# A new instruction order, the last g split in place, and late output copies and transfers shared out, in an attention and two-MLP kernel

## The chip, the core and the metric

One core of a Trainium2 chip runs the whole program. The metric is the device time of one execution in microseconds; several runs give a median. TensorE is called PE, VectorE DVE, ScalarE ACT, GpSimd POOL and SyncE SP.

## What is computed

Three stages follow each other, all in float32. Attention of 4 batches, 8 heads, 576 positions and 64 columns is the sum of a coarse part (means of 4 positions, softmax over 144 of them, each result repeated 4 times) and a local part (softmax over the 7 positions within 3 of the query). Its output, 2304 rows of 512, goes through

```python
def _moe_ref(x, w1, w2, w3, w_out):
    a = x @ w1
    b = x @ w2
    h = a * b @ w3
    return (h @ w_out)

def _moe2_ref(x, w1, w2, w3, w_out):
    h = np.maximum(np.maximum(x @ w1, x @ w2), x @ w3)
    return (h @ w_out)
```

with inner widths 1024 and 768. The weights arrive as float64 words and are converted on the chip.

## The kernel before, in words

**Tiling.** The 2304 rows are five chunks of N = 504 (the last has 288). Products split each operand into a rounded high part and a rest (split, lines 447 to 453: ACT makes the high part, DVE the rest) and are three matmuls (mm3, lines 455 to 458). The first stage loads and converts w_out and w3 and multiplies them (weights_product; float32 at lines 476 to 482 is one ACT and four DVE operations; the product is line 750), while down (lines 505 to 600) makes the coarse attention of one pair of heads and slab the local one. Then front and back do the first MLP chunk by chunk, halves_front and rest_front the second MLP's three products with a running maximum, and final_rest and final its last product. halves_front works on two chunks at a time, rest_front on the chunk of 288; both store their maximum g to memory (g_dram), from where final and final_rest load it. z of rest_front is zs[2], in a buffer of its own that nothing uses again.

**The end.** final(ch) takes a chunk of 504 in two halves of columns, with seven products in place of eight and sums of them on DVE (t1, u2, t5, u3). put copies a result into output tiles whose columns are interleaved: one copy for each run of positions, each output tile T = 384 columns for one row group j, one half of the batches rd and one l of four. l = 0, 1 are the low tiles, 2, 3 the high ones. When the last copy into a tile is added, put adds its transfer (line 1002), 192 KB each, on SP's queue. In final the copies run on ACT. The last chunk's last product is cut into u = 0 and 1, both into one PSUM bank b1 (252 columns each); put for each has six copies of 12, 12, 96, 96, 24 and 12 columns, alternately on ACT and DVE (line 1107):

```python
for u in low:
    product(0, 2, x21, b1, False, (u,))
    put(b1, t0, n, [u], 0, u * n, ("ACT", "DVE"))
```

**The order.** Nothing is emitted where the code computes it. prog.add collects tasks (engine, cost, tiles read and written) and numbers them from 0; a tile may be given with a part, and then only accesses to the same part or to the whole tile depend on each other. ORDER, a table at the top, holds for each engine the task numbers in the order in which its queue runs them. Program.order simulates this with rough costs (AFTER: time from an engine's end to those who wait; RATE: bytes per us of the transfers; HAND, COME: PE's instructions at hand and their supply; PAUSE, HEAT: PE's clock), to choose among free buffers, and so decides which task is emitted next: the one that can start first. Each engine runs its queue in order; semaphores between the queues are set by the framework from the tiles that the emitted instructions touch, in the order of emission.

**Names used below.** Tasks 0 to 7 are warm-up matmuls (line 500). 20 is the first pair's scores (line 540); 221 and 222 load the two halves of the first part of w_out, 228 the first half of w3; 224 to 227, 231 to 234 and 236 to 239 are their DVE conversions; 315 is the first product of weights (line 750). For the second batch, 455 and 482 normalise the exponentials of head pairs 0 and 1 (line 570, ACT), 459/457 and 485/483 are pp and dp work (transposes on PE, line 579, copies on ACT, line 582; 457, 459 the copies of pair 0, 483, 485 the transposes of pair 1), 460 is the values product of pair 0 (line 589); 480 and 481 are DVE's sums and reciprocals of pair 1; 489 loads q and k of pair 2, and 497, 498 copy them (line 523, ACT). 609, 611, 615, 617 are the first four front products, 621 to 624 the first back products. At the end, before the change, 2557 and 2567 are the last product's u = 0 and 1, 2568 to 2576 the copies and transfers of u = 1 (2573 is the 24 columns on ACT, 2575 the last 12 on DVE); after it, they are 2547 and 2557, with 2558 to 2566, and 2542, 2544 and 2546 are the transfers of the high tiles.

## Time and profile before

| | us |
|---|---|
| three runs, lowest / median / highest | 746.69 / 749.17 / 751.23 |
| the profiled execution, its own time | 745.55 |
| its span, first to last instruction | 743.8 |
| PE busy in the span | 724.7 |
| DVE busy | 506.4 |
| ACT busy | 339.4 |

The span is 1.75 us shorter than the execution's own time. "Idle" and "waits" say how long an engine stood before an instruction and what ended that; busy times of PE are modelled from the records.

### The profile page before, as it was taken

The numbers are of one execution on the slowest core, as the hardware profiler recorded it, in microseconds if no ns is written. First come the engines' busy times: TensorE is split into PE (matmuls) and PEld (weight loads), VectorE is DVE, ScalarE is ACT, GpSimd is POOL, SyncE is SP. The second block draws the span as 40 slices with busy tenths as digits, with TensorE's granted clock in tenths as the row PEclk, the third lists the DMA queues.
The fourth block names the chain that finished last, engine by engine and source line by source line (L and its number), as shares of the span: only waits on it lengthen the run. The fifth ranks groups of instructions, "written<-read, shape, count | busy, mean of one in ns | idle before, by whom it ended". The sixth has DMA issues, their size and how long they took to land.

```text
span 743.8 us, 16204 instructions
## 1 busy us (share of the span) xinstructions
PE 724.7 (97%) x6636; PEld 578.0 (78%) x6636; DVE 506.4 (68%) x859; ACT 339.4 (46%) x744; POOL 48.6 (7%) x114
## 2 busy tenths in 40 slices
PE   6999999999999999999999999999999999999995
PEld 2445567777877777777888899888888888879995
DVE  6999988866253544354577699979846765468983
ACT  4865586555644573322443466432212311114775
POOL 2410104010310300000000000000000000000000
PEclk9999999999999999999999999999999999999998
DMA  9887854222432322012566496778593588586416
GB/s 333 277 248 228 262 175 109 84 50 68 104 82 68 64 75 60 21 34 53 186 238 253 173 309 226 271 265 273 221 363 111 196 286 269 200 295 225 143 46 223
DMA packets 64489, 133.31 MB, mean 179 GB/s; under 512 B 23520, under 2 KB 44000, under 8 KB 61344
## 3 DMA queue, kind: packets, MB, share of 16 engines
q1 hardware_dynamic: 59808, 128.74, 51.3%
q0 software_dynamic: 4608, 3.55, 3.4%
q8 instruction: 52, 0.85, 0.5%
q14 instruction: 21, 0.17, 0.1%
HBM read 90.57 MB, written 41.68 MB: 178 GB/s over the span
## 4 chain that ended last, share of the span: by engine, by line
PE 86%; DVE 8%; DMA 2%; ACT 1%; issue 1%; SPq 0%; DVEq 0%; ACTq 0%
PE pb L456 12%; PE pb L457 11%; PE pb L458 11%; PE pf L456 9%; PE pf L458 9%; PE pf L457 9%; PE py L456 5%; PE py L457 5%; PE py L458 5%; PE pw L750 3%; PE poq L688 2%; PE sq L643 2%; DVE wf L480 2%; DVE wf L482 1%; PE po L589 1%
## 5 line engine op out<-in xcount | busy, mean ns | idle before, releaser
L456 PE MATMUL pf<-xt,w 128*128 128x504 f32 (+1 forms) x320 | 121.0, 378 | 0.8 <-ACT dp L582 0.8
L456 PE MATMUL pb<-xc,wu 128*128 128x504 f32 (+1 forms) x324 | 120.7, 373 | 0.5
L457 PE MATMUL pb<-xc,wu 128*128 128x504 f32 (+1 forms) x324 | 119.8, 370 | 0.0
L458 PE MATMUL pb<-xc,wu 128*128 128x504 f32 (+1 forms) x324 | 119.5, 369 | 0.0
L458 PE MATMUL pf<-xt,w 128*128 128x504 f32 (+1 forms) x320 | 118.8, 371 | 0.0
L457 PE MATMUL pf<-xt,w 128*128 128x504 f32 (+1 forms) x320 | 118.8, 371 | 0.0
L456 PEld LDWEIGHTS pb<-xc,wu 128*128 128x128 f32 x324 | 60.8, 188 | 14.6 <-DVE t L912 4.7
L456 PEld LDWEIGHTS pf<-xt,w 128*128 128x128 f32 x320 | 60.1, 188 | 12.0 <-ACT dp L582 1.5
L458 PEld LDWEIGHTS pb<-xc,wu 128*128 128x128 f32 x324 | 60.9, 188 | 10.2
L457 PEld LDWEIGHTS pb<-xc,wu 128*128 128x128 f32 x324 | 60.9, 188 | 9.7
L458 PEld LDWEIGHTS pf<-xt,w 128*128 128x128 f32 x320 | 60.1, 188 | 10.4
L457 PEld LDWEIGHTS pf<-xt,w 128*128 128x128 f32 x320 | 60.2, 188 | 9.6
L782 DVE TENSOR_TENSOR z<-pf,z 128x504 f32<-128x504 f32 (+1 forms) x40 | 25.4, 635 | 60.0 <-PE pf L458 48.1
L912 DVE TENSOR_TENSOR t<-t,pb 128x504 f32<-128x504 f32 x60 | 40.4, 677 | 38.0 <-PE pb L458 19.9
L914 ACT COPY t<-pb 128x504 f32<-128x504 f32 x36 | 20.9, 581 | 97.8 <-PE pb L458 93.7
L456 PE MATMUL py<-g,wp 128*128 128x504 f32 (+1 forms) x160 | 63.6, 397 | 0.0
L750 PE MATMUL pw<-wf 128*128 128x512 f32 x128 | 58.8, 604 | 4.0 <-DVE wf L482 4.0
L457 PE MATMUL py<-g,wp 128*128 128x504 f32 (+1 forms) x160 | 59.5, 372 | 0.0
L458 PE MATMUL py<-g,wp 128*128 128x504 f32 (+1 forms) x160 | 59.4, 371 | 0.0
L456 PE MATMUL pb<-go,wm 128*128 128x252 f32 x168 | 46.9, 279 | 1.3 <-ACT area L996 1.3
L458 PE MATMUL pb<-go,wm 128*128 128x252 f32 x168 | 46.9, 279 | 0.0
L457 PE MATMUL pb<-go,wm 128*128 128x252 f32 x168 | 46.8, 278 | 0.0
(136 smaller groups left out, 1306.2 us busy)
## 6 DMA issues: line engine op xcount, KB each, us to landing
wu<-w_dram SPq DMA_DIRECT2D x18, 1024.0 KB, 7.6
w_dram<-hl SPq DMA_DIRECT2D x20, 512.0 KB, 3.0
qk<-qkp SPq DMA_DIRECT2D x16, 576.0 KB, 3.8
raw<-m SPq DMA_DIRECT2D x18, 512.0 KB, 3.7
raw<-w3t SPq DMA_DIRECT2D x16, 512.0 KB, 11.5
raw<-w SPq DMA_DIRECT2D x16, 512.0 KB, 4.5
w_dram<-hls SPq DMA_DIRECT2D x16, 512.0 KB, 3.6
m_dram<-hls SPq DMA_DIRECT2D x12, 512.0 KB, 5.4
```

What stands on the lines that cost most here:

```text
L456: nc.tensor.matmul(o, wlo, xhi, start=first, stop=False, skip_group_check=again)
L457: nc.tensor.matmul(o, whi, xlo, start=False, stop=False, skip_group_check=again)
L458: nc.tensor.matmul(o, whi, xhi, start=False, stop=last, skip_group_check=again)
L480: prog.add(dve(n), lambda e: e.scalar_tensor_tensor(u(), high(), 0xC0000000, u(), op0=ALU.bitwise_and, op1=ALU.bitwise_or), [words], cv)
L482: prog.add(dve(n), lambda e: e.scalar_tensor_tensor(u(), low(), 29, u(), op0=ALU.logical_shift_right, op1=ALU.bitwise_or), [words], cv)
L589: e.matmul(po()[a * D:(a + 1) * D, :GD], vd()[:, k, a * D:(a + 1) * D], pt()[:, k, a], start=(k == 0), stop=(k == 1),)
L643: e.matmul(sps[a]()[j * 32:(j + 1) * 32, (half * HP + hp) * BK:(half * HP + hp + 1) * BK], q[h, t:t + 32], k[h, t:t + BK], start=True, sto ...
L688: e.matmul(pos[hp]()[a * D:(a + 1) * D, i * BQ:(i + 1) * BQ], vw()[h, a, i], pt().rearrange("p a n -> p (a n)")[h, c:c + BQ], start=True, ...
L750: e.matmul(os[i](), w()[:, i * P:(i + 1) * P], o(), start=n == 0, stop=n == NF - 1)
L782: prog.add(psum(n), lambda e, pp=pp: e.tensor_tensor(z()[:, :n], pp()[:, :n], z()[:, :n], op=ALU.mult), [pp], [z])
L912: prog.add(dve(N), lambda e: e.tensor_tensor(ap(o), ap(x), ap(y), op=op), [x, y], [o])
L914: copy = lambda o, x: prog.add(act(N), lambda e: e.copy(ap(o), ap(x)), [x], [o])
```

## The change

It replaces ORDER on all engines (the task numbers from 2268 on shift, since ten transfers go), changes five constants of the planner, no longer stores and reloads g of f = 2 and 5 for the chunk of 288 but splits it from zs[2], shares put's copies of the last chunk between ACT and DVE, makes copies of b1 depend on half of it (part = u, also for the product that writes it), and stores the two high tiles of a row group with one transfer of 384 KB, from POOL's queue in the second half of the batches and from SP's in the first.

```diff
@@ ORDER["PE"] @@
-    "0 20 1 2 3 4 315 5 6 31 7 29 47 316 124 317 33 318 125 56 58 74 319 320 60 83 85 101 321 87 135 322 159 110 "
...
-    "615 617 621 622 460 623 624 625 627 485 631 632 633 483 634 501 635 637 641 551 642 643 644 552 645 487 510 "
...
-    "2408 2415 2423 2431 2462 2464 2466 2468 2474 2481 2491 2524 2526 2528 2530 2536 2543 2557 2567",
+    "0 1 20 2 3 4 5 315 6 29 7 31 47 316 124 317 33 318 125 58 56 74 319 320 60 83 85 101 321 135 87 322 159 112 "
...
+    "110 160 114 331 137 332 138 170 194 333 195 334 172 335 173 336 447 205 337 207 338 208 458 456 474 609 611 "
+    "615 617 460 483 485 621 622 623 624 625 627 631 501 632 633 634 635 551 637 641 552 642 643 644 487 512 645 "
...
+    "2404 2411 2419 2426 2457 2459 2461 2463 2469 2476 2484 2517 2519 2521 2523 2529 2536 2547 2557",
@@ ORDER["DVE"], its first and last lines @@
-    "18 19 236 237 22 21 238 239 224 225 231 226 227 232 233 234 248 249 250 251 26 27 45 241 46 242 243 244 269 "
...
-    "2507 2511 2475 2469 2476 2482 2513 2514 2516 2520 2518 2521 2529 2531 2523 2537 2538 2544 2565 2559 2561 "
-    "2569 2575 2571",
+    "18 19 236 22 237 238 21 231 232 239 233 234 224 225 226 227 248 45 249 26 27 250 46 251 241 242 243 244 49 "
...
+    "2503 2500 2504 2470 2471 2477 2506 2507 2511 2509 2513 2514 2522 2516 2524 2528 2530 2531 2535 2526 2533 "
+    "2537 2545 2539 2549 2555 2565 2541 2559 2551 2561",
@@ ORDER["ACT"], around tasks 455 and 482, and its last lines @@
...
-    "443 444 200 360 356 354 471 371 470 176 206 180 450 451 452 367 365 498 455 211 217 213 382 459 457 497 341 "
-    "219 343 339 477 478 376 479 610 524 345 613 616 525 387 378 389 619 393 482 400 461 626 486 398 629 484 404 "
-    "504 505 506 415 411 636 409 426 509 557 639 646 488 513 511 531 532 533 536 656 563 515 431 538 649 540 592 "
...
-    "2542 2551 2546 2547 2558 2535 2560 2563 2554 2548 2539 2545 2541 2573 2568 2570",
...
+    "282 130 82 61 86 303 104 105 84 106 289 136 88 109 325 323 329 113 111 327 115 296 310 165 349 141 444 145 "
+    "171 470 200 443 360 471 354 176 356 180 206 450 451 452 367 365 371 455 382 217 211 459 341 457 610 339 477 "
+    "478 479 345 343 482 378 616 389 376 613 387 619 497 393 498 461 404 486 626 524 484 504 505 525 506 398 409 "
+    "629 509 219 636 411 213 400 415 639 513 488 557 646 426 649 511 563 531 532 422 533 536 656 538 592 515 540 "
...
+    "2360 2518 2472 2295 2485 2515 2407 2492 2421 2410 2473 2312 2302 2525 2305 2474 2534 2527 2475 2491 2543 "
+    "2550 2532 2548 2553 2560 2558 2540 2563 2538",
@@ ORDER["POOL"], ORDER["SP"] @@
...
+    "1046 1048 1071 1124 1098 1125 1102 1100 1101 1099 1126 1072 2544 2546 2542",
-    "8 222 9 221 228 245 246 229 35 266 267 252 253 36 259 260 63 62 89 273 90 274 280 301 281 302 288 287 436 "
...
-    "2485 2484 2493 2552 2553 2562 2566 2564 2556 2550 2576 2574 2549 2555 2572",
+    "8 222 9 228 246 221 245 35 266 229 267 253 252 36 259 63 260 62 89 273 90 274 117 280 118 123 281 287 302 "
...
+    "2433 2269 2496 2495 2498 2494 2493 2497 2431 2430 2481 2487 2424 2479 2486 2490 2489 2556 2554 2566 2562 "
+    "2552 2564",
@@ -248,12 +248,12 @@
-    AFTER = {"PE": 0.16, "DVE": 0.12, "ACT": 0.15, "POOL": 0.15, "SP": 1.9}
-    RATE = 0.36e6
+    AFTER = {"PE": 0.16, "DVE": 0.12, "ACT": 0.15, "POOL": 0.15, "SP": 2.3}
+    RATE = 0.33e6
     ADDS, MORE = 2.2, 4.5
 
-    HAND, COME = 165, 70
-    BEGIN, PAUSE, HEAT = 0.8, 4.2, 4.5
+    HAND, COME = 165, 45
+    BEGIN, PAUSE, HEAT = 0.8, 3.8, 4.5
 
     def __init__(self):
         self.tasks, self.chains, self.group = [], {}, 0
@@ -967,14 +967,14 @@
                 prog.add(act(n), lambda e, i=i, pp=pp: e.copy(z()[:, i], pp()[:, :n]), [pp], [(z, i)])
             else:
                 prog.add(dve(n), lambda e, i=i, pp=pp: e.tensor_tensor(z()[:, i], z()[:, i], pp()[:, :n], op=ALU.max), [pp], [(z, i)])
-            if w == 2:
+            if w == 2 and p < HF - 1:
                 f = p + i * HF
                 dma(lambda f=f: g_dram[f]()[:, (NW - 1) * N:], lambda i=i: z()[:, i], [(z, i)], [(g_dram[f], NW - 1)], P * n * 4)
 
 
     outs = {}
 
-    def put(src, t0, n, ls, stride, at=0, on=("ACT",)):
+    def put(src, t0, n, ls, stride, at=0, on=("ACT",), part=None):
         runs = {}
         for m in range(t0 // TT, (t0 + n) // TT):
             q, h = divmod(m, 2)
@@ -993,29 +993,39 @@
             got = lambda u0=u0, ni=ni: view(src(), at + u0 * TT, [[stride, len(ls)], [2 * TT, ni], [1, TT]])
             tiles = [(o[l % 2][0], (b, s, h, i0)) for l in ls]
             if on[i % len(on)] == "ACT":
-                prog.add(("ACT", 0.09 + 0.0019 * len(ls) * w), lambda e, dst=dst, got=got: e.copy(dst(), got()), [src], tiles)
+                prog.add(("ACT", 0.09 + 0.0019 * len(ls) * w), lambda e, dst=dst, got=got: e.copy(dst(), got()), [(src, part)], tiles)
             else:
-                prog.add(dve(len(ls) * w), lambda e, dst=dst, got=got: e.tensor_copy(dst(), got()), [src], tiles)
+                prog.add(dve(len(ls) * w), lambda e, dst=dst, got=got: e.tensor_copy(dst(), got()), [(src, part)], tiles)
             for l in ls:
                 o[l % 2][1] += w
-                if o[l % 2][1] == T:
-                    dma(lambda rd=rd, j=j, l=l: out[rd * NJ + j, l], lambda o=o[l % 2][0]: o(), [o[l % 2][0]], [], P * T * 4)
+            if ls[0] >= KX // 2 and all(c == T for _, c in o):
+
+                prog.add(("POOL", 1.0) if rd == NR - 1 else ("SP", 0.43), lambda e, rd=rd, j=j, o=o[0][0]: e.dma_start(
+                    out[rd * NJ + j, KX // 2:].rearrange("l p t -> p l t"), view(o(), 0, [[T, 2], [1, T]])),
+                    [t for t, _ in o], [], size=P * T * 8)
+            elif ls[0] < KX // 2:
+                for l in ls:
+                    if o[l][1] == T:
+                        dma(lambda rd=rd, j=j, l=l: out[rd * NJ + j, l], lambda o=o[l][0]: o(), [o[l][0]], [], P * T * 4)
 
     def load_g(t, at, f, ch):
         n = WIDTHS[ch]
         dma(lambda: at(t), lambda: g_dram[f]()[:, ch * N:ch * N + n], [(g_dram[f], ch)], [(t, f)], P * n * 4)
 
-    def final_rest(ch, gplaces, stage, ms):
+    def final_rest(ch, gplaces, stage, ms, z):
         prog.group += 1
         n = WIDTHS[ch]
         g = []
         for f in range(NF2):
-            st = stage.tile([P, n], F32, "gf")
-            load_g(st, lambda st: st(), f, ch)
+            kept = f % HF == HF - 1
+            if not kept:
+                st = stage.tile([P, n], F32, "gf")
+                load_g(st, lambda st: st(), f, ch)
+            got = (lambda i=f // HF: z()[:, i]) if kept else (lambda st=st: st())
             if f % 2 == 0:
                 g.append(Tile(gplaces[f // 2], [P, 2, 2, n], F32R, "gg"))
             t = g[-1]
-            split(lambda t=t, f=f: t()[:, f % 2, 0], lambda t=t, f=f: t()[:, f % 2, 1], lambda st=st: st(), n, [st], t)
+            split(lambda t=t, f=f: t()[:, f % 2, 0], lambda t=t, f=f: t()[:, f % 2, 1], got, n, [(z, f // HF)] if kept else [st], t)
         for l in range(KX):
             prog.group += 1
             pp = Tile(everywhere, [P, 512], F32, "pb")
@@ -1061,7 +1071,8 @@
                         mm3(pp()[:, u * n:(u + 1) * n], w[:, i, 0, c], w[:, i, 1, c], x()[:, 0, f], x()[:, 1, f],
                             first and f == u == 0, f == HF - 1, u == 1 or not first)
 
-            prog.add(mm(n, 9 * len(us)), products, [x, *(m[j] for m in ms)], [pp], chain="x")
+            to = [pp] if len(us) == 2 else [(pp, us[0])]
+            prog.add(mm(n, 9 * len(us)), products, [x, *(m[j] for m in ms)], to, chain="x")
 
         flat = lambda x: x()[:, :N]
 
@@ -1081,6 +1092,7 @@
         tt(b21, b21, b11, ALU.subtract)
         v4 = keep(b21)
         low, high, t0 = [0, 1], [2, 3], ch * N
+        both = ("ACT",) if ch < NW - 2 else ("ACT", "DVE")
         product(0, 0, x11, b1, True)
         copy(t1, b1)
         product(1, 0, v1, b3, True)
@@ -1089,14 +1101,14 @@
         add(u2, t1, b2)
         product(1, 3, x22, b3, False)
         add(u2, u2, b3)
-        put(u2, t0 + n, n, low, n)
+        put(u2, t0 + n, n, low, n, on=both)
         product(1, 2, v3, b2, False)
         add(u3, t1, b2)
         add(t5, u3, t5)
-        put(t5, t0 + n, n, high, n)
+        put(t5, t0 + n, n, high, n, on=both)
         product(0, 3, v4, b4, True)
         add(u3, u3, b4)
-        put(u3, t0, n, high, n)
+        put(u3, t0, n, high, n, on=both)
         if ch < NW - 2:
             product(0, 2, x21, b1, False)
             put(b1, t0, n, low, n)
@@ -1104,7 +1116,7 @@
 
         for u in low:
             product(0, 2, x21, b1, False, (u,))
-            put(b1, t0, n, [u], 0, u * n, ("ACT", "DVE"))
+            put(b1, t0, n, [u], 0, u * n, both, u)
 
     def attention(b):
         for hp in range(HP):
@@ -1214,7 +1226,7 @@
     in_slots = lambda slots: [lambda s=s: parts(s, 2, T) for s in slots]
     halved = lambda slots: [lambda ps=ps, i=i: ps[i:i + 2] for s in slots for ps in [parts(s, 4, T)] for i in (0, 2)]
     out_places = [in_slots(tqr.slots) + halved([last[1], stage[0]]), in_slots(gr.slots + cvr.slots) + halved([last[0]])]
-    final_rest(NW - 1, [*tqr.slots, place[2]], Ring(x32r.slots + odr.slots[1:]), ms)
+    final_rest(NW - 1, [*tqr.slots, place[2]], Ring(x32r.slots + odr.slots[1:]), ms, zs[2])
     stage_g = Ring([vws[0], place[3], place[10], place[2]])
     ops, temps = Ring([place[9], place[0], *kq, place[5], place[11]]), Ring(zr.slots + orr.slots + loose + z_slots)
     for ch in range(NW - 1):
```

## Rows read from the trace of the kernel before

**Rows 1.** The page's head: span, and busy time of each engine with its share.

```profile
span 743.8 us, 16204 instructions
...
PE 724.7 (97%) x6636; PEld 578.0 (78%) x6636; DVE 506.4 (68%) x859; ACT 339.4 (46%) x744; POOL 48.6 (7%) x114
```

**Rows 2.** Stages: length, busy time of PE, PEld, DVE, ACT, POOL; clock, DMA share, GB/s.

```profile
0.00:10.00 10.00, 6.14 (x14) 2.67 (x15) 4.28 (x10) 3.29 (x5) 4.02 (x19) 1.00 0.81 271
10.00:93.00 83.00, 78.07 (x1008) 39.38 (x1007) 79.84 (x131) 54.82 (x118) 14.25 (x37) 1.00 0.85 270
93.00:734.50 641.50, 639.05 (x5607) 534.89 (x5605) 421.25 (x714) 278.36 (x608) 30.33 (x58) 1.00 0.51 165
```

**Rows 3.** Waits of PE over the whole span: us in total, times, longest.

```profile
PE pw L750 <- DVE wf L482: 4.0, 3, 2.3
PE sp L540 <- DVE qs L530: 2.5, 1, 2.5
...
PE pb L456 <- ACT area L996: 1.3, 1, 1.3
...
PE pb L456 <- ACT gg L449: 0.7, 1, 0.7
```

**Rows 4.** ACT at 93 us, and PE's first front product, in order of time.

```profile
93.67 1.21 ACT L523 COPY area<-qk 128x576 f32<-128x576 f32 x1 [2.33 <-DMA qk<-qkp]
94.78 1.33 ACT L570 ACTIVATE e<-e,two 72x144 f32<-72x144 f32 x4
...
98.26 0.50 PE L456 MATMUL pf<-xt,w 128*128 128x504 f32 x1 [0.83 <-ACT dp L582]
```

**Rows 5.** PE in order of time: its last gap, ahead of the last product.

```profile
735.95 0.38 PE L456 MATMUL pb<-go,wm 128*128 128x252 f32 x1 [1.27 <-ACT area L996]
```

**Rows 6.** DVE, then ACT, in order of time: output copies from bank pb.

```profile
734.71 0.47 DVE L998 COPY area<-pb 128x12 f32<-128x12 f32 x3 [0.37 <-PE pb L458]
737.36 0.18 DVE L998 COPY area<-pb 128x12 f32<-128x12 f32 x1 [2.17 <-PE pb L458]
737.80 0.40 DVE L998 COPY area<-pb 128x12 f32<-128x12 f32 x2 [0.27 <-ACT area L996]
...
735.27 0.18 ACT L996 COPY area<-pb 128x12 f32<-128x12 f32 x1
...
735.51 0.38 ACT L996 COPY area<-pb 128x96 f32<-128x96 f32 x2
...
737.57 0.20 ACT L996 COPY area<-pb 128x24 f32<-128x24 f32 x1 [0.63 <-DVE area L998]
738.23 0.39 ACT L996 COPY area<-pb 128x12 f32<-128x12 f32 x2 [0.46 <-DVE area L998]
```

**Rows 7.** The last output transfers: two stretches, issues from 734 us (landing), SP's last five.

```profile
736.00:742.50 6.50, 1.25 (x9) 1.05 (x9) 0.58 (x3) 1.53 (x7) 0.00 (x0) 0.79 0.94 343
742.60:743.80 1.20, 0.00 (x0) 0.00 (x0) 0.00 (x0) 0.00 (x0) 0.00 (x0) 0.50 0.00 0
...
out<-area SPq DMA_DIRECT2D x12, 192.0 KB, 2.1
...
738.65 2.30 SPq L424 DMA_DIRECT2D out<-area  x5
```

**Rows 8.** Transfers issued by POOL before: line 515, size, us from issue to landing.

```profile
vd<-vp POOLq DMA_DIRECT2D x15, 72.0 KB, 2.9
...
L515 POOL DMA_DIRECT2D vd<-vp x15: 832/835/1177, 24.3 to 250.3; - x15
...
DMA to landing us min/median/max: 2.5/2.9/9.1
```

**Rows 9.** ACT in order of time: the split of the last g.

```profile
668.43 0.43 ACT L449 CAST gg<-gf 128x288 fp32r<-128x288 f32 x1 [6.73 <-DMA gf<-g_dram]
```

**Rows 10.** ACT, then PE, in order of time: head pair 1 of the second batch.

```profile
113.15 1.32 ACT L570 ACTIVATE e<-e,two 72x144 f32<-72x144 f32 x4
...
109.35 0.39 PE L456 MATMUL py<-g,wp 128*128 128x504 f32 x1
...
118.42 0.41 PE L579 MATMUL pp<-ident,e 72*72 72x72 f32 x4
```

177 rows, old and new, of the table ORDER are left out of this document.

## The prediction, made before the change was run

> **What bounds the kernel now.** I read the page's first part, then the span by stages, then PE's waits, then the last 10 us engine by engine. PE is busy for 97% of the span [rows 1]. From 93 to 734.5 us it misses 2.5 us of 641.5, so nothing in that stretch can give much; in the first 10 us it misses 3.9, and from 10 to 93 us another 4.9, while DVE is busy for 79.8 of these 83 us: there the weights' conversion on DVE sets the pace [rows 2]. PE's largest waits are few [rows 3]: for the converted weights (4.0 us in 3 waits), for the first sums of q and k (2.5), for ACT in the last output copies (1.3) and for the last split of g (0.7). With the 0.83 us at 98.26 [rows 4] these are 9.3 us, and a new order can win only what it takes from them, and from the 6.5 us after the last matmul, which ends at about 737.3.
>
> **The last product.** u=1 of the last product waits 1.27 us for ACT [rows 5]: put's copies of u=0 read the bank that it writes into, and the planner took them as readers of the whole tile. With part=u the planner no longer makes the product wait. It emits the task that can start first; u=1 can start when u=0 ends, the copies 0.16 us later (AFTER), so the product now stands ahead of u=0's copies in the program. -1.27 us on PE. But the copies are then behind it. What do they cost? In the rows the two engines never copy out of that bank together: DVE 737.36, ACT 737.57, DVE 737.80, ACT 738.23, each waiting for the other's end, though ACT's 24 columns (task 2573) and the 12 that DVE takes next (2575) go to different output tiles [rows 6]. So the bank as a whole is handed over, and u=0's six copies (1.2 us, 734.71 to 735.89) and u=1's six (1.3 us, 737.36 to 738.6) come one after the other from 736.0 on: 736.0 + 0.1 + 2.5 = 738.6, where they end today. Bounds: 737.4 (six on each engine side by side, no longer than u=1's six) and 739.7 (twelve hand-overs of 0.3 us, the time of the widest copies). I take 738.6, nearest to how they run now.
>
> The Trainium skill (PSUM — Partial Sum Buffer, section "PSUM bank collisions raise a hardware error") says that no two engines may touch one bank's quadrant at once, whatever the columns, and that semaphores must guard the bank, not the address. That speaks against part=u and agrees with the hand-overs of rows 6; by it the sum below stays; a split that did work by halves would end the copies at 737.4 and win 1.2 us more.
>
> **The last transfers.** The last twelve output tiles (192 KB each, 2.36 MB) are issued from 734.8 on and keep the DMA engines 94% busy at 343 GB/s from 736 to 742.5; five are issued after the last copy, in 2.3 us, each lands 2.1 us after its issue, and 1.2 us follow without any [rows 7]. Merging the high halves takes three issues off SP's tail and puts them on POOL, but the bytes are the same, and after the last copy 3 SP tiles and one POOL pair remain, again five tiles. At that rate their 0.98 MB take 2.9 us, however many queues hold them. The copies of u3, which feed the three POOL transfers, are shared by ACT and DVE, but the new order runs the widest (192) after those of the low half, so these transfers start no sooner. POOL issues in 0.83 us and 72 KB land after 2.9 us in the median, 2.5 to 9.1 [rows 8]; the spread shows what a busy DMA does to it. I take 0 for the whole end of the kernel, copies and transfers together, and keep both ends: -0.9 (SP's last issue comes two places sooner) and +5.1 (a POOL pair that lands 9.1 us after the last copy, where SP's last tile today lands after 4.0); midway between median and slowest, 6.0 us, it is +2.0.
>
> The Trainium skill (DMA: Bandwidth & Descriptors, "Anatomy of one DMA — SWDGE (gpsimd) path") fits a POOL transfer as 2.0 us plus its bytes at 436 GB/s: an estimated 2.9 us for the 393 KB pair. By it the POOL pair would land a microsecond before today's last tile, SP's tiles would decide, and the sum would be -2.4 in place of -1.5; no row here has a transfer of that size on POOL.
>
> Sharing the t copies with DVE costs nothing on PE: DVE copies 12 and 96 columns in 0.40 us [rows 6] and has idle time between its last adds; u3's add may come later by one such copy, which only its own copies notice.
>
> **The last g.** ACT idles 6.73 us until the load of f=5 lands, at 668.43 [rows 9], and PE waits 0.7 us for this split [rows 3]. Taken from zs[2], which is complete before the last unit's halves, store, load and wait go: -0.7 us (bounds 0 and -0.7). Next in line is the split of the first go operand, which is wanted only after twelve more products. Two stores and two loads of 144 KB also leave SP and the DMA.
>
> **The order.** Up to the first weights product nothing is won: it needs the same 16 DVE operations before it in both orders; w_out's half 0 is loaded two places later but converted last, so the wait for it is covered by other DVE work. The second warm-up task now stands ahead of the first scores and fills part of the 2.5 us, but one less stands behind. At 93.67 ACT has idled 2.33 us for the q/k load of head pair 2 of the second batch (copy 498 behind load 489), with the normalising of pair 0 (task 455) queued behind it; through pp and dp that is PE's 0.83 us before the first front product [rows 4]. In the new ACT order 455 is ahead and 498 comes 24 places later: -0.8 us (bounds 0 and -0.8). All else that moved I take at 0: it stands beside a busy PE. Its ends: -3.0 (the other two waits for weights and the small ones) and +5.3 (below).
>
> Sum: 0 - 0.7 - 0.8 + 0 = -1.5 us. The profiled execution took 745.55 (span 743.8), so 744.05 for one like it; the runs' median, 749.17, lies 3.6 us above, and I carry the same difference over: **747.7 us**.
>
> **Rivals.**
> Faster: the 3.6 us between the profiled execution and the median are in no trace. If they are late loads in the first 93 us, where the DMA share is 0.81 to 0.85 [rows 2] and DVE sets the pace, then an order searched with slower transfers (RATE 0.33e6, 2.3 us after each) absorbs them: converted halves stand later behind their loads, as w_out's half 0 does. 747.7 - 3.6 = 744.1. Against it: DVE's 3.2 us of idle time in this stretch are small in the trace, and a new order has waits of its own. Chance 0.25.
>
> Slower: the new PE order puts pair 1's two transposes (483, 485) straight behind the fourth front product and pair 0's values (460), with all of back's first group behind them in the queue. Today back starts at 109.35, after four front products in 11.1 us, and the transposes run from 118.42 on, filled around by products; their exponentials are normalised only at 113.15 to 114.47 [rows 10]. The front products start at 97.4 in the new order, so PE reaches 483 at 97.4 + 11.1 + 0.65 = 109.2. ACT needed 18.4 us from 455 to the normalising of pair 1 (task 482) with 26 tasks between [rows 4, 10]; 13 of them now come later, so about 9 us less, which should do. If the chain through DVE (480, 481) doesn't follow, PE stands for up to 114.5 - 109.2 = 5.3 us: 747.7 + 5.3 = 753.0, at the edge of what can be told; it decides from 5.2 us on, so only if the chain has gained nothing, and any wait that it causes behind itself puts it clearly past. Chance 0.10.
>
> The change doesn't do at the end what it says: PE still waits for the copies, or the POOL pair lands last and late. 747.7 + 1.3 = 749.0 for the first, 747.7 + 2.0 = 749.7 for the second. Chance 0.15.
>
> **How the numbers follow.** The forecast has 0.50. A measurement of this kernel can tell about 0.5% (3.7 us) from no change: faster is below 745.4, slower above 752.9. Faster takes the first rival and a little of the forecast's lower end: 0.28. Slower takes the second: 0.10. Same: 0.62. The range runs from 744.0, just inside the faster rival, to 751.7, past the late POOL pair (749.7) with a stall of 2 us on top; it leaves out the stalls of 4 us and more and the orders that also win at the start.
>
> **What would show it.** Right: no PE wait before the last product; twelve copies from the bank handed to and fro after the last matmul, ending near 738 on the scale of today's span; DMA engines near full until 1.2 us before the end; no PE wait for gg; ACT's task 455 before the q/k wait. Wrong: PE waits of over 2 us between 95 and 125 us (the slower rival), copies of u=0 beside the last product, or an end 2 us nearer to the last matmul than the 6.5 us of today plus the 1.3 us that the product gains.

## The result, and the profile after

The changed kernel takes 755.16 us in the median of 6 runs (753.49 to 756.82), the kernel before 749.17 on the same chip: a ratio of 1.0087 [1.0059, 1.0114]. It is slower by 6.0 us, outside the range and by more than the 0.5% that can be told. The profiled execution took 753.49 us, its span 751.7 us, 7.9 us over the span before [rows 1]. The page's head:

```profile
span 751.7 us, 16174 instructions
...
PE 728.7 (97%) x6636; PEld 580.8 (77%) x6636; DVE 508.4 (68%) x866; ACT 338.7 (45%) x737; POOL 52.8 (7%) x117
```

PE is busy for 4.0 us more with the same 6,636 matmuls. The last of them ends at 740.77 us (before: 737.25), and the tail behind it is 10.95 us (before: 6.50). So 3.5 us were lost up to PE's end and 4.4 behind it.

**The first 93 us.** PE's waits over the span (us in total, times, longest):

```profile
PE pw L750 <- DVE wf L482: 4.8, 4, 2.1
PE poq L688 <- DMA area<-v: 2.9, 1, 2.9
...
PE pp L579 <- DVE x L697: 0.6, 1, 0.6
```

The waits for gg and for ACT's output copies are gone from the list [rows 3], as predicted; the second row is new: 2.9 us for a load of v's weights. The chain that ended last, 50 to 73 us (start, us, what), shows where it comes from:

```profile
51.50 0.68 PE po L589 x8
...
52.20 0.31 SPq L515
...
52.55 5.32 DMA raw<-w3t
...
57.89 7.20 DMA area<-v
...
65.22 1.30 PE poq L688 x57
66.53 6.05 PE pw L750 x8
```

The load was issued at 57.89, landed after 7.2 us, and PE's poq had waited for it since 62.3. It is the last of five that stand on SP behind a v load, vd<-vp (task 463); by this chain its issue also waited for a raw weight of w3t, likewise behind the v load, that landed at 57.87. SP in order of time:

```profile
47.14 0.90 SPq L424 DMA_DIRECT2D area<-vl  x2
52.20 0.31 SPq L515 DMA_DIRECT2D vd<-vp  x1
52.55 1.30 SPq L424 DMA_DIRECT2D raw<-w3t  x3
53.90 1.66 SPq L424 DMA_DIRECT2D area<-v  x3
...
56.21 2.01 SPq L424 DMA_DIRECT2D area<-v  x2
```

Between 48.1 and 52.2 SP issues nothing: the v load waits there for PE (po), and three raw weights of w3t and the five loads wait with it. The wait of PE isn't all. The same stretch in windows (length, busy time of PE, PEld, DVE, ACT, POOL; clock, DMA share, GB/s):

```profile
55.00:64.50 9.50, 7.28 (x158) 3.89 (x156) 9.15 (x13) 4.87 (x9) 0.00 (x0) 1.00 0.90 246
64.50:71.40 6.90, 6.18 (x66) 3.40 (x67) 3.20 (x6) 0.63 (x1) 0.83 (x1) 0.51 0.87 269
```

While PE stood, the granted clock fell from its higher level (2.4 GHz) to the lower (1.2 GHz); it stayed there for 6.9 us, in which eight pw matmuls took 6.05 us, against 3.70 for eight at 47.4 us.

**The end.** DVE's and ACT's copies and POOL's and SP's issues, in order of time on each engine:

```profile
740.81 0.18 DVE L998 COPY area<-pb 128x12 f32<-128x12 f32 x1 [1.10 <-PE pb L458]
741.38 0.18 DVE L998 COPY area<-pb 128x12 f32<-128x12 f32 x1 [0.39 <-ACT area L996]
...
742.48 0.56 DVE L998 COPY area<-pb 128x12 f32<-128x12 f32 x3 [0.18 <-ACT area L996]
...
742.30 0.54 ACT L996 COPY area<-t 128x192 f32<-128x192 f32 x1
743.07 0.20 ACT L996 COPY area<-pb 128x24 f32<-128x24 f32 x1 [0.23 <-DVE area L998]
743.15 0.23 ACT L996 COPY area<-t 128x24 f32<-128x24 f32 x1
...
740.35 0.79 POOL L1003 DMA_DIRECT2D out<-area  x1 [455.98 <-ACT area L996]
743.14 1.46 POOL L1003 DMA_DIRECT2D out<-area  x2 [2.00 <-DVE area L998]
...
741.58 2.89 SPq L424 DMA_DIRECT2D out<-area  x6
```

The first copy out of the last product's bank starts 0.04 us after PE's last matmul, DVE and ACT take turns at the bank until 743.27, and u3's widest copy (192 columns) and its 24 columns stand between and behind these copies on ACT's queue, until 743.38. POOL, idle for 2.0 us, issues its last two pairs only from 743.14 on. What this means for the transfers is seen in GB/s over the last 16 us in 40 slices of 0.4 us; first the kernel before, then the changed one:

```profile
GB/s 269 223 0 296 365 376 365 361 357 330 300 373 357 376 77 0 0 0 0 161 357 373 353 369 376 399 392 369 292 261 376 411 376 365 373 296 0 0 0 0
```

```profile
GB/s 369 369 369 369 365 342 12 0 0 0 0 0 0 0 0 380 380 311 365 373 365 365 353 288 342 419 300 411 346 369 342 192 0 0 0 0 0 0 0 0
```

Each ends with a full-speed block of some 17 slices: the last twelve tiles. Before, the block starts 1.9 us ahead of PE's end (735.4 against 737.25), and four empty slices (1.6 us) follow it. In the changed kernel it starts at 741.7, 0.9 us after PE's end, and eight empty slices (3.2 us) follow. The block is as long as before; it moved by 2.8 us against PE's end, and with the 1.6 us behind it that is the tail's 4.4.

What fills the empty slices is the program's closing line, where each engine ends with a DRAIN (count; shortest, median and longest in ns; first and last start). First the kernel before, then GpSimd and SP in the changed one:

```profile
L1323 POOLq DRAIN  x3: 45/106/4836, 280.5 to 743.5; - x3
```

```profile
L1335 POOLq DRAIN  x3: 46/93/7290, 743.7 to 751.4; - x3
L1335 SPq DRAIN  x3: 7/7/7, 749.2 to 751.2; - x3
```

Before, GpSimd's long DRAIN stands at 280.5 us, far from the end. Now it runs from 743.65 to 750.94, 2.1 us past the landing of GpSimd's last pair (743.88 + 4.9), and the span ends 0.78 us behind it. SP's first DRAIN stands at 749.17; the kernel before ended 0.83 us behind the same point of SP, which would be 750.0 here. By this count GpSimd's DRAIN alone makes the end 1.7 us later.

### The profile page after: what moved, and what is told of

It is laid out like the page before. It is cut to its first block, busy times and chain, and to the rows that moved or that the text cites. A ratio compares the mean times of both kernels' runs of the same rounds, so it can differ in the third digit from the quotient of the medians.

```text
span 751.7 us, 16174 instructions
## 1 busy us (share of the span) xinstructions
PE 728.7 (97%) x6636; PEld 580.8 (77%) x6636; DVE 508.4 (68%) x866; ACT 338.7 (45%) x737; POOL 52.8 (7%) x117
## 4 chain that ended last, share of the span: by engine, by line
PE 90%; DVE 5%; DMA 2%; issue 1%; ACT 0%; POOL 0%; POOLq 0%; SPq 0%; ACTq 0%; DVEq 0%
PE pb L456 12%; PE pb L458 12%; PE pb L457 12%; PE pf L456 9%; PE pf L458 9%; PE pf L457 9%; PE py L456 5%; PE pw L750 5%; PE py L457 4%; PE py L458 4%; PE poq L688 3%; PE sq L643 2%; PE po L589 1%; PE sp L540 1%; DVE wf L480 1%; DVE wf L482 1%
## 5 line engine op out<-in xcount | busy, mean ns | idle before, releaser
L458 PEld LDWEIGHTS pb<-xc,wu 128*128 128x128 f32 x324 | 60.9, 188 | 10.3
L750 PE MATMUL pw<-wf 128*128 128x512 f32 x128 | 61.3, 624 | 4.8 <-DVE wf L482 4.8
L750 PEld LDWEIGHTS pw<-wf 128*128 128x128 f32 x128 | 24.0, 197 | 32.2 <-issue 25.5
L458 PE MATMUL pb<-go,wm 128*128 128x252 f32 x168 | 46.8, 279 | 0.0
L456 PE MATMUL pb<-go,wm 128*128 128x252 f32 x168 | 46.8, 279 | 0.0
```

What stands on the lines that cost most here:

```text
L456: nc.tensor.matmul(o, wlo, xhi, start=first, stop=False, skip_group_check=again)
L458: nc.tensor.matmul(o, whi, xhi, start=False, stop=last, skip_group_check=again)
L750: e.matmul(os[i](), w()[:, i * P:(i + 1) * P], o(), start=n == 0, stop=n == NF - 1)
```

## The experiments

The ratios are to the kernel before on the same chip, with 95% intervals; its medians were 747.35 us in the first group of four, 747.70 in the second, 747.48 in the third, 746.87 in the last. In experiment kernels the lines stand one or two further down (L516 for L515). The tails, all from the profiled executions (first issue: that of the first of the last twelve tiles):

| run | ratio [95%] | PE's end | first issue ahead of it | tail | first issue to span's end |
|---|---|---|---|---|---|
| before | 1 | 737.25 | 2.48 | 6.50 | 8.98 |
| after | 1.0087 [1.0059, 1.0114] | 740.77 | 0.42 | 10.95 | 11.37 |
| pairs_sp | 1.0071 [1.0045, 1.0098] | 739.69 | 0.99 | 8.80 | 9.79 |
| early_loads | 1.0076 [1.0049, 1.0102] | 738.46 | 0.42 | 10.90 | 11.33 |
| old_order | 1.0016 [0.9996, 1.0036] | 738.10 | 0.43 | 10.14 | 10.56 |
| old_order_sp | 1.0017 [1.0001, 1.0033] | 736.01 | 1.00 | 9.27 | 10.28 |
| v_load_later | 1.0037 [1.0017, 1.0056] | 735.36 | 0.42 | 10.92 | 11.34 |
| three_fixes | 1.0013 [0.9994, 1.0032] | 740.14 | 0.99 | 9.04 | 10.04 |
| pool_early | 1.0009 [0.9991, 1.0026] | 735.63 | 0.42 | 9.71 | 10.13 |
| g_split_only | 0.9980 [0.9964, 0.9995] | 738.46 | 2.49 | 6.46 | 8.94 |
| part_only | 1.0008 [0.9991, 1.0025] | 739.17 | 0.96 | 8.81 | 9.77 |
| two_banks | 0.9971 [0.9955, 0.9988] | 735.30 | 0.95 | 7.99 | 8.94 |
| one_bank_wait | 0.9996 [0.9980, 1.0011] | 737.47 | 2.59 | 6.65 | 9.24 |
| two_banks_new | 1.0035 [1.0017, 1.0053] | 741.56 | 0.99 | 8.28 | 9.27 |

**The order undone.** All tasks of the changed kernel in the order of before (old_order), and with SP's pairs as well (old_order_sp):

```diff
 "PE", and so on in every queue, in the new numbers
-"0 1 20 2 3 4 5 315 6 ..."
+"0 20 1 2 3 4 315 5 6 ..."
```

> The changed kernel's tasks in the order of the kernel before, on every engine; its parts are kept (the split of the last g where it is computed, the product by halves, the copies of the last chunk on two engines, the last pairs by GpSimd). Theory (the order's loss lies in the first 104 us, the parts' loss at the end with GpSimd): TensorE ends at 735 to 736, the tail stays 9 to 11 us long, 748 to 750 us. Rival (the parts cost TensorE time as well): TensorE ends at 738 or later and the time is over 752 us.

> As the run before it, with the three last pairs issued by SyncE. Theory: TensorE ends at 735 to 736 and the tail is 6.5 us as in the kernel before, so 746 to 747.5 us, 2 to 3 us under the kernel before, and 2.5 to 4 us under the run with GpSimd's pairs. Rival (parts worth nothing, the copies set the end wherever the transfers go): 749 us within 1, and the same as the run with GpSimd's pairs.

748.33 and 748.35 us. So most of the loss is the order's, and the rest of the change brings nothing even in the old order. GpSimd's share was misjudged: the tail with SP's pairs is 9.27 us, not 6.5 (with GpSimd's 10.14), and the medians are the same with both queues.

**The late load.** Two tries: the five loads go ahead of the v load (early_loads), or the v load alone goes back (v_load_later).

```diff
 "SP", early_loads
-"... 147 153 463 308 295 309 116 121 120 381 122 119 151 ..."
+"... 147 153 116 121 120 122 119 463 308 295 309 381 151 ..."
 "SP", v_load_later
-"... 147 153 463 308 295 ... 435 462 154 ..."
+"... 147 153 308 295 ... 435 463 462 154 ..."
```

> The changed kernel with one edit in SyncE's order: the five loads of the v weights of the first slab (116 121 120 122 119) go ahead of the v load that waits for TensorE (463) and of three raw weights (308 295 309). Theory (the wait of 2.94 us of TensorE at 65 us for one of these loads, and the half clock that follows it for 6.8 us, are nearly all that the new order loses in the first 104 us): no wait over 0.7 us at 65, the granted clock stays at 1.0 from 60 to 75, TensorE ends 5 to 7 us earlier, 748.5 to 750.5 us. Rival (the new order loses in many places, TensorE just waits for the next late load instead): a wait of 1.5 us or more turns up between 55 and 105 us and the time stays over 753 us.

> The changed kernel with one number moved in SyncE's order: the v load 463, which waits for TensorE, goes from ahead of three raw weights and six other loads to just ahead of 462. Theory (this one waiting transfer is what makes the weights behind it late): no wait of TensorE over 0.8 us between 55 and 75 us, the granted clock at a half for at most 3.4 us after the first 15 us, TensorE ends at 735 to 738, 748.5 to 751 us. Rival (the early loss of the new order is spread over many moves): a wait of 1.3 us or more stays between 55 and 105 us, 752 us or more.

With the five loads ahead, 751.63 us, between both expectations: the raw weights behind the v load became the next late ones, and PE waited 1.50 us at 64 us; the ratio (1.0076) cannot be told from the changed kernel's. With the v load moved, 749.34 us: no stretch at the lower clock level between 10.5 us and PE's end in the profile, that end 5.4 us earlier, and the only PE wait over 0.8 us between 55 and 75 us one of 1.31 us at 68.5, on DVE, which the rival had asked for, though not with this time. The interval [1.0017, 1.0056] lies clear of the changed kernel's. SP then goes on where it had stood:

```profile
47.18 0.90 SPq L425 DMA_DIRECT2D area<-vl  x2
48.12 1.92 SPq L425 DMA_DIRECT2D raw<-w3t  x3
50.08 3.53 SPq L425 DMA_DIRECT2D area<-v  x3
```

**The same move in the kernel before.**

```diff
 "SP" of the kernel before
-"... 287 436 155 122 ... 462 463 187 ..."
+"... 287 436 463 155 122 ... 462 187 ..."
```

> The kernel before with one number moved in SyncE's order: the v load 463, which waits for TensorE, from just behind 462 to just behind 436, ahead of all loads of the weights of v. Theory (a transfer that waits for TensorE at the head of SyncE's queue is the early loss of the change): TensorE waits 2 us or more in one piece between 50 and 75 us, the granted clock falls to a half behind it, 3 to 6 us over the kernel before of the same chip. Rival (the kernel before has slack for it): no wait over 1 us there, within 1.5 us of the kernel before.

752.87 us, 1.0076 [1.0047, 1.0105]: one number in SP's order costs nearly what the whole change does. Its PE waits, and the stretch behind the first of them:

```profile
PE poq L690 <- DVE wf L479: 4.4, 1, 4.4
PE pw L752 <- DVE wf L484: 3.0, 3, 1.5
```

```profile
60.00:69.10 9.10, 4.71 (x37) 2.10 (x25) 5.20 (x9) 2.47 (x5) 0.00 (x0) 1.00 0.79 246
69.10:75.90 6.80, 6.27 (x125) 3.80 (x126) 6.63 (x14) 1.13 (x1) 0.00 (x0) 0.50 0.98 312
```

The wait is for a raw weight this time, and the clock falls behind it as in the changed kernel. That the v load causes the early loss is shown from both sides.

**The end: queue or copies?** The pairs by SP alone (pairs_sp); the v load, the pairs and u3's copies put right (three_fixes); the same with GpSimd's pairs (pool_early).

```diff
-prog.add(("POOL", 1.0) if rd == NR - 1 else ("SP", 0.43), ...
+prog.add(("SP", 0.43), ...                       # pairs_sp, three_fixes
 "ACT"   # three_fixes, pool_early
-"... 2543 2550 2532 2548 2553 2560 2558 2540 2563 2538"
+"... 2543 2540 2538 2550 2532 2548 2553 2560 2558 2563"
 "DVE"
-"... 2545 2539 2549 2555 2565 2541 2559 ..."
+"... 2545 2539 2541 2549 2555 2565 2559 ..."
```

> The changed kernel with one edit: its three last 384 KB transfers are issued by SyncE instead of GpSimd, order otherwise kept. Theory (the end costs time because GpSimd's transfers land late and GpSimd is then drained: 2.9 us from the last landing to the end of the span against 1.2 before): the last transfer lands at about 747.5 of the profile and the span ends about 1.2 us after it, so the time falls by 3 to 4 us, 751 to 752 us. Rival (the end is longer because of the copies handed to and fro between ScalarE and VectorE, whatever the queue): no change, 755 us within 1. TensorE ends as in the changed kernel, near 740.8, under both.

> The changed kernel with three edits: the v load 463 later on SyncE as in the run before it, the last three pairs issued by SyncE, and the copies of u3 (2540, 2538 on ScalarE, 2541 on VectorE) ahead of the copies of the low tiles. Theory (these are the causes): TensorE ends at 735 to 738, the tail is 8 to 9 us, 746 to 748.5 us, no slower than the kernel before. Rival (the new order is slower in other places, or the tail stays at 10 us whatever its queue): 750 us or more.

> As the run with three fixes, but with the last three pairs by GpSimd as in the change: the v load later, the copies of u3 ahead of the low tiles' copies. Theory (GpSimd costs twice: its transfers start late, for which the order of the copies is to blame, and it is drained after their landing): tail 9.8 to 10.5 us, 0.7 to 1.5 us over the run with three fixes. Rival (only the late copies cost): tail 9 us, the same time as with three fixes within 0.4 us.

753.17, 748.80 and 747.44 us. With the copies late, SP shortens the tail by 2.15 us (10.95 to 8.80), not by the 3 to 4 expected, and the ratio by less than the intervals can tell apart (1.0087 to 1.0071). With the copies early the ratios are the same (1.0013 with SP, 1.0009 with GpSimd), but their intervals are too wide to exclude the 0.7 us by which the tails differ (9.04 and 9.71), so the times decide nothing here. The traces say more. In pool_early GpSimd's DRAIN is again the last to end, though SP's tiles are the last to land:

```profile
L1336 POOLq DRAIN  x3: 46/106/7199, 737.3 to 745.1; - x3
```

In all six profiles with GpSimd's pairs its long DRAIN takes 7.2 to 7.3 us, ends 2.1 us after the last pair's landing, and the span ends 0.8 us later. Counted from SP's first DRAIN as above, this makes the end 0.6 us later in pool_early, 1.3 in old_order and 1.7 in the four others. So GpSimd costs time at the end in each of them, most where its transfers are the last to start; no run's time is precise enough to confirm it. The three landings of the pairs in the changed kernel:

```profile
DMA to landing us min/median/max: 3.0/3.9/4.9
```

The Trainium skill (DMA: Bandwidth & Descriptors, "Anatomy of one DMA — SWDGE (gpsimd) path") gives an estimated 2.9 us for such a pair; the first, issued into idle DMA engines, agrees (3.0), the two that share them with SP's tiles don't.

**The parts alone.** The old order and SP's pairs, with the g split and the merged pairs only (g_split_only); the halves added (part_only); the halves in two banks instead (two_banks).

```diff
 # part_only, against g_split_only
-put(b1, t0, n, [u], 0, u * n, ("ACT", "DVE"))
+put(b1, t0, n, [u], 0, u * n, ("ACT", "DVE"), u)      # and product writes (pp, us[0])
 # two_banks, against g_split_only
+b1s = [b1, Tile(everywhere, [P, 512], F32, "pb") if ch == NW - 2 else b1]
-put(b1, t0, n, [u], 0, u * n, ("ACT", "DVE"))
+put(b1s[u], t0, n, [u], 0, u * n, ("ACT", "DVE"))     # product and t1's copy by half
```

> The tasks of the changed kernel without the product by halves' own banks, without VectorE's share of the last copies and without GpSimd's transfers: what is left of the change is the split of the last g where it is computed and one transfer for two high tiles, on SyncE, in the order of the kernel before. Theory (the split's wait of 0.7 us is saved, fewer issues at the end): 0.5 to 1.5 us under the kernel before of the same chip. Rival (the split's wait is absorbed elsewhere): within 0.4 us of the kernel before.

> The kernel of the run with the g split alone, and the product by halves added as the change has it: both halves stay in one bank, the second half is no longer made to wait for the first half's copies. Theory (the copies of the first half then wait for the second half, because they read the same bank): the wait of 1.27 us is gone and TensorE ends earlier, the first copy starts within 0.1 us of TensorE's end, the tail grows from 6.5 to 8 us or more, 0 to 1.5 us over the run with the g split alone. Rival (the halves run apart, as the change says): the tail stays at 6.5 us and the time falls by 1.0 to 1.3 us.

> The kernel of the run with the g split alone, with the two halves of the last product in two PSUM banks, so that neither waits for the other. Theory: the copies of the first half run under the second half's product, TensorE's wait of 1.27 us is gone, the tail stays near 6.5 us, 0.8 to 1.3 us under the run with the g split alone. Rival (the transfers set the end, the DMA engines being busy from the first tile on): the tail grows by what TensorE saves, the same time within 0.4 us.

746.19, 747.60 and 745.36 us. The halves in one bank do what the theory said: PE's 1.27 us are saved, the first copy starts 0.04 us after PE's end at 739.17, and the tail grows by 2.35 us, 1.1 us more than was saved. That the copies wait is the work of the semaphores, which the framework sets by the tile, here the whole bank. DVE's copies out of the bank, first part_only, then two_banks:

```profile
739.21 0.47 DVE L1000 COPY area<-pb 128x12 f32<-128x12 f32 x3 [1.42 <-PE pb L460]
740.38 0.18 DVE L1000 COPY area<-pb 128x12 f32<-128x12 f32 x1 [0.70 <-ACT area L998]
740.83 0.39 DVE L1000 COPY area<-pb 128x12 f32<-128x12 f32 x2 [0.27 <-ACT area L998]
```

```profile
734.29 0.49 DVE L1000 COPY area<-pb 128x12 f32<-128x12 f32 x3 [0.37 <-PE pb L460]
735.34 0.48 DVE L1000 COPY area<-pb 128x12 f32<-128x12 f32 x3 [0.55 <-PE pb L460]
```

In two banks the first half's copies run under the second half's product (734.29, PE's end 735.30). Still the tail is 7.99 us, not 6.5: it grows by what PE saves, as the rival said. The time is 0.8 us lower than g_split_only's (0.9971 against 0.9980), within the intervals, and decides between neither. GB/s of g_split_only, part_only and two_banks, again the last 16 us:

```profile
GB/s 177 311 4 138 369 372 365 357 376 365 349 369 369 380 365 250 0 0 0 27 357 372 365 365 357 369 388 388 380 361 376 353 365 423 376 277 0 0 0 0
```

```profile
GB/s 0 184 369 376 369 338 380 357 361 369 361 388 361 211 0 0 0 77 369 369 169 0 323 373 373 388 242 349 384 369 365 357 372 400 392 231 0 0 0 0
```

```profile
GB/s 200 292 0 157 380 372 361 342 380 369 349 373 369 380 361 231 0 0 0 31 369 384 350 365 365 369 403 384 380 361 376 365 361 388 400 250 0 0 0 0
```

In g_split_only and two_banks the block is the same; in part_only one pair goes out, then the engines run dry before the low tiles come. In the table, the five kernels whose block SP issues alone and without such a hole (before, g_split_only, two_banks, one_bank_wait, two_banks_new) need 8.9 to 9.3 us from the first issue to the end; the four with SP alone and a hole (pairs_sp, old_order_sp, three_fixes, part_only) 9.8 to 10.3; the five with GpSimd's pairs 10.1 to 11.4, without a hole, since their data flow 1.3 us behind the first issue, not 0.85, and GpSimd's DRAIN follows. So with SP alone and no hole the end is first issue plus about 9 us: 2.36 MB at about 370 GB/s are 6.4 us, and start and landing the rest. By this, what PE saves behind the first issue is worth nothing; the times above don't contradict it.

**The halves undone in the new order.** one_bank_wait is three_fixes without the halves; two_banks_new gives it two banks.

```diff
 # one_bank_wait, against three_fixes
-put(b1, t0, n, [u], 0, u * n, both, u)
+put(b1, t0, n, [u], 0, u * n, both)
-to = [pp] if len(us) == 2 else [(pp, us[0])]
+to = [pp]
 "DVE"
-"... 2541 2549 2555 2565 2559 2551 2561"
+"... 2541 2555 2549 2551 2565 2559 2561"
 "SP"
-"... 2554 2566 2562 2552 2564"
+"... 2554 2552 2566 2562 2564"
 # two_banks_new, against one_bank_wait: b1s as in two_banks
```

> The run with three fixes, and the product by halves undone as well: the second half waits again for the first half's copies, and these are put in VectorE's and SyncE's order ahead of the second half's. Kept of the change: its order, the g split, the copies on two engines, the pairs in one transfer. Theory (what is left of the change's loss is that the first half's copies come after the last product, so the transfers start later against TensorE's end and pause): a wait of 1.0 to 1.4 us of TensorE before its last product, the first transfer is issued 2 us or more before TensorE's end, the tail falls from 9.0 to 7 us or less, 0.5 to 2 us under three_fixes, 0.996 to 0.999 of the kernel before. Rival (the new order is slower elsewhere): no gain over three_fixes, 1.001 or more.

> The same kernel with the halves of the last product in two banks: no wait, and the first half's copies under the second half's product. Theory: TensorE ends 1 to 1.3 us earlier than in the run before it, the tail is 7 to 8 us since the transfers keep the DMA engines busy from the first on, 0 to 1 us under the run before it, 0.995 to 0.998 of the kernel before: the best of all. Rival (transfers alone set the end): the same as the run before it.

745.99 us (0.9996): PE's wait is back and the tail shrinks from 9.04 to 6.65 us.

```profile
PE pb L457 <- ACT area L997: 1.3, 1, 1.3
```

two_banks_new took 749.49 us, 1.0035 [1.0017, 1.0053], and is a miss: the fifth bank isn't free in this order when PE wants it (second row below), and its profiled execution waited longer for the converted weights, with three stretches at the lower clock level in the first 77 us.

```profile
PE pw L751 <- DVE wf L483: 6.8, 3, 4.2
...
PE pb L457 <- ACT area L997: 0.8, 1, 0.8
```

**One that tells nothing.** The old order for the tasks below 1549 only:

```diff
 ORDER: in every queue the numbers below 1549 in the sequence of before, all others kept
```

> The changed kernel with the order of the kernel before for the tasks below 1549 (all engines, about the first 230 us of the work), the new order for all others, GpSimd's last pairs kept. Theory (the order loses only in the first 104 us): TensorE ends at 736 to 738, the tail stays near 11 us, 748 to 750.5 us. Rival (the order after that loses as well): 752 us or more, TensorE's end at 739 or later.

754.73 us, 1.0101 [1.0077, 1.0124]. The start is good (no wait over 2.3 us, first front product at 99.95 us), but where the two orders meet, at 382 us, PE waits 3.3 us for a split, and 6.8 us at the lower clock level follow. The seam costs what was to be measured.

```profile
PE py L458 <- DVE g L452: 3.8, 2, 3.3
```

## Why the prediction was wrong

**Where the loss lies.** In ratios: the v load 0.0050 (1.0087 to 1.0037), u3's late copies 0.0028 (to 1.0009, with GpSimd's pairs), the halves 0.0017 (1.0013 to 0.9996), together 7 us. The sum leaves out the step from GpSimd's queue to SP's (1.0009 to 1.0013), which the ratios cannot tell from 0. Only the first step's intervals lie apart; the other two rest on their tails as well (10.92 to 9.71; 9.04 to 6.65 for 1.34 us of wait). What is left, at 0.9996, cannot be told from g_split_only.

**The step that failed: the order.** "All else that moved I take at 0: it stands beside a busy PE." The v load 463 stands beside a busy PE and waits for it, on SP's queue, ahead of three raw weights and five loads of v's weights that PE needs soon. I had followed the queues of ACT and PE past each moved step, but on SP only for the weights' halves. The term was 0, with ends of -3.0 and +5.3 us; measured it is +3.7 us (0.0050). In the two profiles PE's end moved by 5.4 us: the wait is 2.9, the low clock some 3 (v_load_later's PE busy time is 725.9 us against 728.7). No other part of the new order can be told from 0. With the v load right the first front product starts at 98.48, 98.72 and 98.87 us in the three profiles without a stretch at the lower clock level ahead of it (v_load_later, pool_early, one_bank_wait), before at 98.26 [rows 4]; in the two with such stretches (three_fixes, two_banks_new) it starts at 103.2 and 103.5, so one profile of each kernel settles no more than this.

**The end.** I took 0, with bounds -0.9 and +5.1; it is about +3.4 us (0.0028 + 0.0017 of 748), inside them. The copies behaved as predicted: those out of the bank are handed to and fro and end 2.50 us after PE's end (predicted 2.6). By the Trainium skill's rule (PSUM — Partial Sum Buffer, "PSUM bank collisions raise a hardware error") they had to be kept apart; the traces agree so far that no copy reads the bank while PE writes into it, and that in two banks copies and product overlap. What failed is the step from there to the transfers. By the prediction's terms the tail is 2.6 us to the last copy, 4.0 from there to the last landing and 1.2 behind it, 7.8 in all (6.5 plus the 1.3 that PE gains). Measured are 2.61 (with u3's last copy), 5.4 and 2.9, 10.95 in all, 3.2 us more.

The middle term: "their 0.98 MB take 2.9 us, however many queues hold them" counts the tiles issued behind the last copy and assumes that the others have gone out before. At the end of the last copy, 743.38, data still flow for 5.0 us, at about 370 GB/s some nine of the twelve tiles, for the block starts only at 741.7. The last term: that the queue doesn't matter was wrong too, since GpSimd's DRAIN ends 2.1 us after its last landing. So the late POOL pair of the third rival came: it lands 5.4 us after the last copy, where the rival took 6.0. That rival's mechanism was right, but its 2.0 us lack the DRAIN, and no rival had the load.

**The last g.** -0.7 us: no run waits for gg, and g_split_only is 0.0020 [0.0005, 0.0036] under the kernel before, 0.4 to 2.7 us. Right in sign; the merged pairs are in that number too, and v_load_early, which keeps the store and the load, shows no wait for gg either, so that not every execution has these 0.7 us to win.

**ACT's q/k wait.** -0.8 us: the wait is gone as said, but pp then waits 0.57 us for DVE in place of it (0.83 before). By these gaps the term is about -0.3 us, which no run can tell from 0.

**The rivals.** The slower one (the transposes 483 and 485) had the right sign and the wrong place: between 95 and 125 us PE waits 0.57 us at most. The faster one, a start without late waits, did not come. The 3.6 us that are in no trace seem to go with the clock: of 29 executions of the kernel before in the third group, the four with a mean granted clock of 0.998 took 744.72 to 745.68 us, the six at 0.992 to 0.994 748.38 to 750.34; the profiled one had 0.997.

## What to carry to other kernels

A transfer that waits for an engine holds up every transfer behind it on its queue: in a new order, list each such transfer and what now stands behind it, and count its wait as theirs. A kernel that ends in a block of transfers which one queue issues without a hole ended here about 9 us after the first issue, so look for what feeds the first transfer and for holes in the block; work saved behind that point buys little. See which engine's closing DRAIN ends last before late transfers go to another queue. The lowest time here, of g split, merged pairs and two banks in the old order, is 745.36 us, 0.9971 [0.9955, 0.9988]; it cannot be told from g_split_only's 0.9980.

## What was not expected of the hardware

The same order can run its start at two clocks. The twelve executions of three_fixes have mean granted clocks from 0.988 (752.07 us) to 0.997 (745.97 us). three_fixes and v_load_later have the same order up to the last chunk; the same stretch in their profiled executions:

```profile
16.50:19.90 3.40, 3.40 (x5) 1.35 (x4) 3.37 (x7) 3.40 (x8) 0.00 (x0) 0.50 1.06 388
```

```profile
16.50:19.90 3.40, 3.40 (x12) 1.49 (x12) 3.37 (x6) 3.40 (x7) 0.30 (x1) 1.00 1.05 386
```

Five matmuls against twelve. Ahead of it PE had waited 3.17 us in one piece in the first and 2.05 in the second. With a second such stretch at 30.1 us in the first, PE ended 4.8 us later there (740.14 against 735.36). Why the waits differ between executions stays open: in both, the DMA engines were busy throughout (1.06 and 1.05). So a small wait at the start costs more than itself, in some executions and not in others, and a single profile of this kernel can be off by 5 us.

GpSimd's DRAIN at the end of a program outlasts the landing of its last transfer by 2.1 us in all six profiles where it issued pairs there, and all other engines wait for it. Why it takes that long stays open.
